# Low parts of the first-layer weights all on GpSimd, and the token-counting products behind the first-layer product

## The chip, the cores and the metric

The kernel runs on one core of a Trainium2 chip. A time is the device's microseconds (us) for one execution; the median of three runs of the kernel before is 858.86 us (857.1 to 858.91). The engines are TensorE (PE; PEld is its loading of weights), VectorE (DVE), ScalarE (ACT), GpSimd (POOL) and SyncE (SP). Each works through its own list of instructions in order; an instruction that waits holds up all that stand behind it on the same engine.

## The reference

Three stages follow each other. The third, to which the change belongs, is:

```python
def _moe2_ref(x, w_gate, w1, w2):          # x 3072x384, 8 experts, w1 384x1024, w2 1024x384
    cap = N // E                           # 384 tokens for each expert
    order = np.argsort(-(x @ w_gate).flatten())
    for idx in order:                      # greedy: best logit first, an expert closes at cap
        tok, e = idx // E, idx % E
        if assigned[tok] >= 0 or counts[e] >= cap: continue
        assigned[tok] = e; counts[e] += 1
    for e in range(E):
        mask = assigned == e
        out[mask] = np.maximum(x[mask] @ w1[e], 0.0) @ w2[e]
```

Ahead of it stand a gated linear attention over 32 heads and 768 positions, and a dense pair of layers (384 to 2048 to 384) with a squared relu.

## The kernel before

Attention and the dense layers fill the first 568 us or so. Then the expert stage begins. Experts are found one after the other: a search (function `search`, line 836) narrows a threshold in five rounds until some expert is full; which one closes next is known only then. The eight experts that are found are called k = 0 to 7, in that order. While expert e is computed, expert k = e + 1 is searched, loaded and prepared.

**Products.** All weights and activations are float32 split in two float32r parts, a high one (a rounded copy) and a low one (the rest); each product is high by high, high by low and low by high. Expert e takes eight steps s. A step is nine first-layer products (`layer1`, L993, 128x384 each, into `ph`), the relu on ACT (L1001) and the low part of its result on DVE (L1002), and nine second-layer products of the step two earlier (`layer2`, L1011, three for each third i of the tokens). The first-layer products take the low parts of the weights as they go: the sixth of the nine is the first to read the low part of the third piece.

**Weights.** For each expert POOL issues an indirect load of w1 (L742, into `w1s`) and w2 (L746, into `w2s`), as soon as the search has named it and the one buffer of each is free. `split_w` (L946) then makes the two parts of seven pieces: 0 to 2 of w1 (128x1024) and 3 to 6 of w2 (128x768). "h" is the high part, on ACT (L956); "p" the low part on POOL and "d" the low part on DVE (both L958).

**Tokens.** `slots` (L767) turns the mask of an expert's tokens into a list of rows, in ten steps: two products that count tokens (L771 and L772, into `pp`, which read the mask `mk` and its running sum `mi`), a chain of small DVE operations (L775 to L783), three DVE comparisons of 128x1024 (`spot`, L790, into `lh`) with small products (L799), 24 small products (L807, into `po`), the row numbers (L811 to L820), and last the gather of the tokens (L764, three indirect DMAs on POOL into `xg`). `expert_x` (L960) transposes the three gathered tiles on PE (L966, "x0" to "x2") and splits them on ACT and DVE (L967, L968).

**Order.** The order of the stage is written out by hand in tables. An entry (r, p, "...") puts operations at place p of step r; r counts steps from the start of the expert before k, so 0 to 7 lie in expert k-1 and 8 to 15 in expert k itself. Places 0 and 1 are around the first-layer products, 2 is behind relu, 3 to 5 follow the three thirds of the second layer. "s" is a step of the search, "t" of `slots`; "e", "w" are the copy and the indirect write of a third of an expert's output (L1016, L1019). `STEADY` orders search and slots of k = 2 to 7, `FIRST` those of k = 1; `EXTRA` the preparation of k = 1 to 5, `EXTRA6` and `EXTRA7` that of k = 6 and 7; `OUT` the output of every expert. The function `side` (L1048) looks them up:

```python
for k, r in ((e + 1, s), (e, s + FT2), (e - 1, s + 2 * FT2)):
    for a in PLAN[3 if k == 1 else min(max(0, k - E + 3), 2)].get((r, p), "").split():
        if a == "s":   next(rest, None)
        elif a == "t": next(SL[k], None)      # where slots of k has begun
        ...
        elif a[0] == "w": write(k, i)
        else: split_w(k, i, a[:-1])
```

Of the kernel before, what the change touches and what calls it, by code (L numbers as in the profile page):

```python
# [41 lines left out]
def table(entries):  # L42
    at = {}
    for r, p, what in entries:
        at[r, p] = at.get((r, p), "") + " " + what
    return at
# [1 line left out]

STEADY = ((0, 0, "s"), (0, 1, "s"), (0, 3, "s"), (0, 4, "s"), (0, 5, "s"), (1, 1, "s"), (1, 3, "s"), (1, 5, "t"),
# [3 lines left out]
OUT = (17, 3, "e0"), (17, 4, "e1"), (17, 5, "e2"), (18, 2, "w0"), (20, 0, "w1"), (20, 5, "w2")  # L55
EXTRA = ((4, 2, "h0"), (4, 4, "h1"), (5, 3, "d0 h2"), (6, 0, "h3"), (6, 3, "x0"), (6, 4, "p2 p1"), (7, 3, "x2 p3"),
         (7, 4, "x1"), (7, 5, "h6"), (8, 0, "h4 p4"), (8, 2, "h5"), (8, 5, "p6"), (9, 2, "p5"))
EXTRA6 = ((5, 2, "h0"), (5, 3, "d0 h1"), (5, 5, "h2 d1"), (6, 2, "d2"), (6, 3, "x0"), (6, 4, "x1"), (6, 5, "x2"),
          (7, 1, "h3"), (7, 2, "h4 d3"), (7, 3, "h5 d4"), (7, 5, "h6 d5"), (8, 0, "d6"))
# [19 lines left out]
         (7, 3, "s"), (7, 4, "s"))  # L79
PLAN = [table(STEADY + OUT + e) for e in (EXTRA, EXTRA6, EXTRA7)] + [table(FIRST + OUT + EXTRA)]  # L80
FL = (2, 2, 1, 2)
# [1214 lines left out]
```

## Time and profile before

| | |
|---|---|
| profiled execution | 860.5 us, of which the span from first to last instruction is 858.7 |
| median of three runs | 858.86 us |
| mean granted TensorE clock | 0.972 |
| PE busy | 799.7 us, 93% of the span |
| DVE, ACT, POOL busy | 499.2, 339.5, 368.1 us |

A share of busy time is a mean over stages. In the expert stage one expert follows the other every 32 to 33 us, and what a change is worth there is read from the places where PE stands still within such a period. Matmuls overlap, so that a group of nine is shown as 1.75 to 1.83 us where the next group begins 1.6 us later.

### The profile page before, as it was taken

The page shows a single profiled execution, that of the slowest core. Times are in us where ns is not written, and L with a number is a line of the kernel's source. Part 1 is how long each engine was busy: PE and PEld are TensorE (multiplying, and loading weights), DVE is VectorE, ACT ScalarE, POOL GpSimd, SP SyncE. Part 2 cuts the span into 40 slices and gives each one's busy share as a digit, 9 for nine tenths or more (in the row PEclk, how much of TensorE's full clock was granted, in tenths as well). Part 3 has the DMA queues.
Part 4 walks back from the last instruction along what each step waited for, and adds up shares of the span by engine and source line. Part 5 has one row for each costly group of instructions (what it writes and reads, how often), then busy time and mean ns, then how long its engine had stood idle before and what let it go on. Part 6 is the DMA issues. An engine that isn't in the chain of part 4 may idle for free.

```text
span 858.7 us, 14480 instructions
## 1 busy us (share of the span) xinstructions
PE 799.7 (93%) x5752; PEld 753.1 (88%) x5752; DVE 499.2 (58%) x1150; ACT 339.5 (40%) x615; POOL 368.1 (43%) x351
## 2 busy tenths in 40 slices
PE   7688899999999999999999999986999899999993
PEld 6588898999999999999999999876788888889993
DVE  8898995444444435435433223476877877877730
ACT  2256463333234333233233345223436536536620
POOL 2355662342343343243242344225467577573411
PEclk9699999999999999999999999996999999999997
DMA  8455423112112112112100000041432522523510
GB/s 262 148 170 169 147 60 96 43 49 70 42 50 70 42 49 70 42 50 80 62 20 28 1 31 5 15 150 44 175 121 83 204 95 108 193 92 121 193 37 31
DMA packets 21627, 75.55 MB, mean 88 GB/s; under 512 B 3137, under 2 KB 10178, under 8 KB 19634
## 3 DMA queue, kind: packets, MB, share of 16 engines
q0 software_dynamic: 5520, 34.61, 11.0%
q1 hardware_dynamic: 11682, 25.72, 9.4%
q10 hardware_dynamic: 4352, 14.24, 5.6%
q8 instruction: 46, 0.75, 0.4%
q14 instruction: 27, 0.22, 0.1%
HBM read 63.84 MB, written 9.54 MB: 85 GB/s over the span
## 4 chain that ended last, share of the span: by engine, by line
PE 76%; DVE 14%; DMA 3%; ACT 3%; issue 2%; POOL 0%; SPq 0%; POOLq 0%; DVEq 0%; ACTq 0%
PE ph L389 22%; PE p L417 20%; PE ph L993 10%; PE py L1011 8%; DVE wbuf L958 3%; PE py L274 3%; PE psc L253 2%; PE p L672 2%; PE py L271 2%; DMA w1s<-in_moe_w_dram,wi 2%; ACT wbuf L956 2%; DMA akq<-in_akq_dram 2%; PE pn L293 1%; DVE suf L226 1%; DVE hl L1002 1%
## 5 line engine op out<-in xcount | busy, mean ns | idle before, releaser
L389 PE MATMUL ph<-xT,wbuf 128*128 128x384 f32 x1152 | 227.2, 341 | 9.9 <-DVE wbuf L460 7.7
L389 PEld LDWEIGHTS ph<-xT,wbuf 128*128 128x128 f32 x1152 | 204.7, 189 | 14.2 <-DVE wbuf L460 10.0
L417 PE MATMUL p<-wbuf,hl 128*128 128x392 f32 (+1 forms) x1008 | 202.3, 344 | 0.0
L401 DVE SCALAR_TENSOR_TENSOR s<-ph,s 128x384 f32<-128x384 f32 x112 | 62.2, 556 | 221.7 <-ACT s L394 221.7
L417 PEld LDWEIGHTS p<-wbuf,hl 128*128 128x128 f32 x1008 | 176.4, 188 | 1.7 <-issue 0.4
L405 POOL TENSOR_TENSOR hl<-s,hl 128x384 fp32r<-128x384 f32 x96 | 97.8, 1019 | 173.8 <-ACT hl L402 148.2
L394 ACT ACTIVATE s<-ph 128x384 f32<-128x384 f32 x128 | 63.1, 493 | 174.5 <-PE ph L389 133.3
L1011 PE MATMUL py<-wbuf,hl 128*128 128x384 f32 x576 | 124.3, 347 | 0.0
L993 PE MATMUL ph<-xt,wbuf 128*128 128x384 f32 x576 | 119.7, 352 | 1.3 <-DVE xt L968 0.9
L993 PEld LDWEIGHTS ph<-xt,wbuf 128*128 128x128 f32 x576 | 101.8, 193 | 4.7 <-DVE xt L968 2.3
L1011 PEld LDWEIGHTS py<-wbuf,hl 128*128 128x128 f32 x576 | 99.5, 189 | 0.1
L1001 ACT ACTIVATE hl<-ph 128x384 fp32r<-128x384 f32 x64 | 31.5, 492 | 113.2 <-PE ph L993 102.7
L402 ACT ACTIVATE hl<-s 128x384 fp32r<-128x384 f32 x96 | 50.4, 525 | 55.9 <-DVE s L401 54.8
L1002 DVE SCALAR_TENSOR_TENSOR hl<-ph,hl 128x384 fp32r<-128x384 f32 x64 | 35.4, 554 | 34.2 <-ACT hl L1001 33.5
L956 ACT ACTIVATE wbuf<-w1s 128x1024 fp32r<-128x1024 f32 x24 | 52.2, 2219 | 3.0 <-DMA w1s<-in_moe_w_dram,wi 3.0
L1019 POOL DMA_INDIRECT out_dram<-o,idx x24 | 30.5, 1270 | 52.0 <-ACT o L1016 18.4
L246 POOL TENSOR_TENSOR sad<-state,ae 48x192 f32<-48x192 f32 x40 | 27.0, 675 | 47.6 <-DVE state L310 36.9
L958 POOL TENSOR_TENSOR wbuf<-w2s,wbuf 128x768 fp32r<-128x768 f32 x24 | 43.7, 1846 | 4.4 <-ACT wbuf L956 4.4
L764 POOL DMA_INDIRECT xg<-x2d,row x24 | 23.0, 957 | 39.1 <-DVE idx L820 14.9
L958 POOL TENSOR_TENSOR wbuf<-w1s,wbuf 128x1024 fp32r<-128x1024 f32 x11 | 33.0, 3032 | 3.1 <-ACT wbuf L956 3.0
L357 POOL TENSOR_TENSOR wbuf<-wf,wbuf 128x384 fp32r<-128x384 f32 x16 | 18.3, 1141 | 37.3 <-ACT wbuf L356 37.2
L226 DVE TENSOR_TENSOR_SCAN suf<-akq,fresh 112x516 f32<-112x516 f32 x24 | 31.8, 1327 | 3.5 <-DMA akq<-in_akq_dram 2.9
(213 smaller groups left out, 1096.0 us busy)
## 6 DMA issues: line engine op xcount, KB each, us to landing
akq<-in_akq_dram ACTq DMA_DIRECT2D x16, 677.2 KB, 4.6
rawi<-in_moe_w_in_dram SPq DMA_DIRECT2D x16, 384.0 KB, 3.1
rawo<-in_moe_w_out_dram SPq DMA_DIRECT2D x16, 384.0 KB, 3.8
akq<-in_akq_dram SPq DMA_DIRECT2D x7, 677.2 KB, 5.8
x2d<-xo SPq DMA_DIRECT2D x24, 192.0 KB, 2.2
v<-in_v_dram ACTq DMA_DIRECT2D x16, 192.0 KB, 2.7
v<-in_v_dram SPq DMA_DIRECT2D x8, 192.0 KB, 5.2
xf<-xf SPq DMA_DIRECT2D x16, 72.0 KB, 3.1
```

Source lines behind the costliest of these rows:

```text
L226: dve.tensor_tensor_scan(back(one(P)), back(one(al)), back(one(fresh)), 1.0, op0=OP.mult, op1=OP.add)
L389: pe.matmul(ph[:, :UT], win[:, wi, kt, fs], XT[u][:, xi, kt, :], start=n == 0, stop=n == 3 * KT - 1)
L394: act.activation(s, ph[:, :UT], AF.Relu)
L401: dve.scalar_tensor_tensor(s, ph[:, :UT], 0.0, s, op0=OP.max, op1=OP.mult)
L402: act.activation(hl[:, 0], s, AF.Copy)
L405: (dve if u == 0 or (u, f) == (NU - 1, FT - 1) else pool).tensor_tensor(hl[:, 1], s, hl[:, 0].bitcast(F32), op=OP.subtract)
L417: pe.matmul(PY[u][t][:, :w], hl[:, si, t * C:(t + 1) * C], wout[:, wi, f, :w], start=f == 0 and n == 0, stop=f == FT - 1 and n == 2)
L956: act.activation(dst[:, 0], src, AF.Copy)
L958: (dve if "d" in e else pool).tensor_tensor(dst[:, 1], src, dst[:, 0].bitcast(F32), op=OP.subtract)
L993: pe.matmul(ph[:, :CAP], wa[:, wi, kt, j, :], xt[:, xi, kt, :], start=n == 0, stop=n == 3 * KT - 1)
L1002: dve.scalar_tensor_tensor(hl[:, 1], ph[:, :CAP], 0.0, hl[:, 0].bitcast(F32), op0=OP.max, op1=OP.subtract)
L1011: pe.matmul(PX[k, i][:, :DM], hl[:, hi_, i * 128:(i + 1) * 128], wb[:, wi, j, :], start=j == 0 and n == 0, stop=j == FT2 - 1 and n == 2)
```

## The change

Only the tables change:

```diff
-STEADY = (... (1, 3, "s"), (1, 5, "t"), (2, 0, "s t"), (2, 1, "t t"), (2, 4, "t"), (3, 3, "s"), (3, 5, "t s"), (4, 0, "t t t t"), ...)
+STEADY = (... (1, 3, "s"), (2, 0, "s"), (2, 1, "t"), (2, 3, "t t"), (2, 4, "t"), (2, 5, "t"), (3, 3, "s"), (3, 5, "t s"), (4, 0, "t t t t"), ...)
-OUT = (17, 3, "e0"), (17, 4, "e1"), (17, 5, "e2"), (18, 2, "w0"), (20, 0, "w1"), (20, 5, "w2")
+OUT = (17, 3, "e0"), (17, 4, "e1"), (17, 5, "e2"), (18, 2, "w0"), (20, 0, "w1"), (22, 2, "w2")
-EXTRA = ((4, 2, "h0"), (4, 4, "h1"), (5, 3, "d0 h2"), (6, 0, "h3"), (6, 3, "x0"), (6, 4, "p2 p1"), (7, 3, "x2 p3"),
+EXTRA = ((4, 2, "h0"), (4, 4, "h1"), (4, 5, "p0"), (5, 2, "p1"), (5, 3, "h2"), (6, 0, "h3 p2"), (6, 3, "x0"), (7, 3, "x2 p3"),
```

The low part of piece 0 of k = 1 to 5 goes from DVE ("d0") to POOL ("p0"); p0, p1 and p2 stand earlier in POOL's list. The last third of an expert's output is written two steps later. For k = 2 to 7 the counting products stand behind the nine first-layer products of step 2 instead of ahead of them, and the DVE work that follows them stands behind L1002 of that step. `FIRST`, which orders k = 1, is not changed, and has its last step of `slots`, the gather, at (6, 1).

POOL's list where k = 1 is prepared (w1s and w2s are the loaded weights, wbuf_65 the split ones of k = 1, xg the gathered tokens):

```order
 L742 DMA w1s<-in_moe_w_dram,wi 128x3072
 L746 DMA w2s<-in_moe_w_dram,wi 128x3072
-L764 DMA xg<-x2d,row 128x384 x3
-L958 TENSOR_TENSOR wbuf_65<-w1s,wbuf_65 128x1024 x2
+L958 TENSOR_TENSOR wbuf_65<-w1s,wbuf_65 128x1024 x3
+L764 DMA xg<-x2d,row 128x384 x3
 L958 TENSOR_TENSOR wbuf_65<-w2s,wbuf_65 128x768 x4
```

Three low parts stand in front of the gather, where the gather stood in front of two. For k = 2 to 5 the gather stays in front:

```order
 L764 DMA xg<-x2d,row 128x384 x3
-L1019 DMA out_dram<-o,idx 3072x384 x2
-L958 TENSOR_TENSOR wbuf_64<-w1s,wbuf_64 128x1024 x2
-L958 TENSOR_TENSOR wbuf_64<-w2s,wbuf_64 128x768 x4
-L742 DMA w1s<-in_moe_w_dram,wi 128x3072
-L746 DMA w2s<-in_moe_w_dram,wi 128x3072
-L1019 DMA out_dram<-o,idx 3072x384
-L764 DMA xg<-x2d,row 128x384 x3
-L1019 DMA out_dram<-o,idx 3072x384 x2
-L958 TENSOR_TENSOR wbuf_65<-w1s,wbuf_65 128x1024 x2
+L1019 DMA out_dram<-o,idx 3072x384
+L958 TENSOR_TENSOR wbuf_64<-w1s,wbuf_64 128x1024 x3
```

There, one of the two output writes has moved from ahead of the low parts to a place behind the first three of them.

DVE's list at step 2 of an expert, where the chain of `slots` begins (x, r, b, lh and rh are its intermediate tiles; hl is the relu's low part):

```order
 L933 TENSOR_TENSOR um<-um,na 128x24
+L1002 SCALAR_TENSOR_TENSOR hl_6334<-ph_6321,hl_6334 128x384
 L775 SCALAR_TENSOR_TENSOR x<-mk,pp 128x24
 L778 TENSOR_SCALAR b<-x 128x24 x2
```

```order
 L799 TENSOR_TENSOR rh<-iopc,b 128x24x2 x3
-L790 TENSOR_TENSOR lh<-r_6329,ioslot 128x1024
-L1002 SCALAR_TENSOR_TENSOR hl_6352<-ph_6334,hl_6352 128x384
-L790 TENSOR_TENSOR lh<-r_6329,ioslot 128x1024
+L790 TENSOR_TENSOR lh<-r_6347,ioslot 128x1024 x2
 L1002 SCALAR_TENSOR_TENSOR hl_6380<-ph_6370,hl_6380 128x384
```

The relu's low part of step 2 stood between the second and third comparison and now stands ahead of the whole chain.

## Rows read from the trace of the kernel before

**Rows 1.** The page: busy time of TensorE, and its granted clock.

```profile
PE 799.7 (93%) x5752; PEld 753.1 (88%) x5752; DVE 499.2 (58%) x1150; ACT 339.5 (40%) x615; POOL 368.1 (43%) x351
...
PEclk9699999999999999999999999996999999999997
```

**Rows 2.** Waits of PE, 620 to 850 us: total, times, longest.

```profile
PE pc L874 <- DVE cm L866: 6.2, 5, 1.3
PE pp L771 <- DVE wi L740: 3.2, 5, 1.0
```

**Rows 3.** Timeline 674 to 692, k = 3: start, us, work, idle before.

```profile
681.01 1.00 POOL L1019 DMA_INDIRECT out_dram<-o,idx  x1 [0.43 <-issue]
...
682.48 2.24 DVE L958 TENSOR_TENSOR wbuf<-w1s,wbuf 128x1024 fp32r<-128x1024 f32 x1
...
684.29 0.69 PE L1011 MATMUL py<-wbuf,hl 128*128 128x384 f32 x3
...
685.19 0.95 DVE L866 TENSOR_TENSOR cm<-m,pc 128x768 bf16<-128x768 f32 x1
...
686.20 0.31 PE L874 MATMUL pc<-oh,cm 128*128 128x32 bf16 x6 [1.23 <-DVE cm L866]
```

**Rows 4.** Timeline 611 to 621.5, where k = 1 is prepared.

```profile
611.66 4.19 ACT L956 ACTIVATE wbuf<-w1s 128x1024 fp32r<-128x1024 f32 x2 [2.08 <-DMA w1s<-in_moe_w_dram,wi]
...
613.15 0.95 POOL L764 DMA_INDIRECT xg<-x2d,row  x1 [6.68 <-DVE steps L901]
...
615.67 0.95 POOL L764 DMA_INDIRECT xg<-x2d,row  x1 [0.30 <-issue]
...
618.47 3.29 POOL L958 TENSOR_TENSOR wbuf<-w1s,wbuf 128x1024 fp32r<-128x1024 f32 x1 [1.86 <-ACT wbuf L956]
618.48 0.69 PE L1011 MATMUL py<-wbuf,hl 128*128 128x384 f32 x3
...
620.66 0.53 PE L966 MATMUL px<-ident,xg 128*128 128x128 f32 x3
```

**Rows 5.** Groups by line, 620 to 850 us: busy us, mean ns, idle before.

```profile
L958 POOL TENSOR_TENSOR wbuf<-w1s,wbuf 128x1024 fp32r<-128x1024 f32 x10 | 30.2, 3050 | 2.0 <-ACT wbuf L956 1.9
```

**Rows 6.** DMA issues, 612.9 to 617 us: KB each, median us to landing.

```profile
xg<-x2d,row POOLq DMA_INDIRECT x3, 3.0
```

**Rows 7.** The tile xg, 600 to 660 us.

```profile
DMA to landing us min/median/max: 2.9/3.3/4.4
```

**Rows 8.** Stretches: us, busy of PE, PEld, DVE, ACT, POOL, clock, DMA, GB/s.

```profile
576.00:580.00 4.00, 1.40 (x10) 0.70 (x9) 2.55 (x5) 4.00 (x3) 3.09 (x4) 1.00 0.76 245
580.00:584.00 4.00, 0.51 (x8) 0.28 (x8) 3.51 (x7) 3.30 (x3) 2.84 (x2) 0.77 0.61 196
584.00:588.00 4.00, 3.38 (x24) 3.23 (x24) 2.22 (x7) 0.84 (x1) 4.00 (x3) 0.50 0.03 12
```

**Rows 9.** Timeline 692 to 708, steps 0 to 3 of the next expert.

```profile
694.12 5.44 POOL L958 TENSOR_TENSOR wbuf<-w2s,wbuf 128x768 fp32r<-128x768 f32 x3 [0.84 <-ACT wbuf L956]
...
700.49 0.17 PE L771 MATMUL pp<-mi,onesb 128*128 128x24 bf16 x1 [0.55 <-DVE wi L740]
...
701.26 0.17 DVE L775 SCALAR_TENSOR_TENSOR x<-mk,pp 128x24 f32<-128x24 bf16 x1
...
702.41 0.49 ACT L1001 ACTIVATE hl<-ph 128x384 fp32r<-128x384 f32 x1 [1.94 <-PE ph L993]
...
706.36 0.55 DVE L1002 SCALAR_TENSOR_TENSOR hl<-ph,hl 128x384 fp32r<-128x384 f32 x1
...
706.97 0.76 PE L807 MATMUL po<-rh,lh 128*128 128x6 bf16 x24
```

**Rows 10.** Line 919 on DVE, 570 to 860 us: ns min/median/max.

```profile
L919 DVE SCALAR_TENSOR_TENSOR ez<-cz,ioe x6: 166/168/557, 602.5 to 764.7; 128x8 f32<-128x8 f32 x6
```

**Rows 11.** DVE, 666 to 668 us.

```profile
666.54 0.56 DVE L919 SCALAR_TENSOR_TENSOR ez<-cz,ioe 128x8 f32<-128x8 f32 x1
```

**Rows 12.** POOL, 659 to 672 us.

```profile
659.83 7.25 POOL L958 TENSOR_TENSOR wbuf<-w2s,wbuf 128x768 fp32r<-128x768 f32 x4
```

More of the change, by code (lines that the diff above doesn't have):

```diff
@@ L46, in table @@
     return at
-STEADY = ((0, 0, "s"), (0, 1, "s"), (0, 3, "s"), (0, 4, "s"), (0, 5, "s"), (1, 1, "s"), (1, 3, "s"), (1, 5, "t"),
[1 row of a table removed]
+STEADY = ((0, 0, "s"), (0, 1, "s"), (0, 3, "s"), (0, 4, "s"), (0, 5, "s"), (1, 1, "s"), (1, 3, "s"), (2, 0, "s"),
[1 row of a table added]
           (4, 4, "s"), (4, 5, "s"), (5, 1, "s s"), (5, 3, "s"), (5, 5, "s"), (6, 0, "s"), (6, 3, "s"), (6, 4, "s"),
           (6, 5, "s"), (7, 1, "s"), (7, 3, "s"), (7, 4, "s"))
-OUT = (17, 3, "e0"), (17, 4, "e1"), (17, 5, "e2"), (18, 2, "w0"), (20, 0, "w1"), (20, 5, "w2")
-EXTRA = ((4, 2, "h0"), (4, 4, "h1"), (5, 3, "d0 h2"), (6, 0, "h3"), (6, 3, "x0"), (6, 4, "p2 p1"), (7, 3, "x2 p3"),
+OUT = (17, 3, "e0"), (17, 4, "e1"), (17, 5, "e2"), (18, 2, "w0"), (20, 0, "w1"), (22, 2, "w2")
+EXTRA = ((4, 2, "h0"), (4, 4, "h1"), (4, 5, "p0"), (5, 2, "p1"), (5, 3, "h2"), (6, 0, "h3 p2"), (6, 3, "x0"), (7, 3, "x2 p3"),
          (7, 4, "x1"), (7, 5, "h6"), (8, 0, "h4 p4"), (8, 2, "h5"), (8, 5, "p6"), (9, 2, "p5"))
```

2 rows, old and new, of the table STEADY are left out of this document.

## The prediction

> **What bounds the kernel now.** I read the page first: TensorE is busy 93% of the span, and its granted clock is full in all but a few slices [rows 1]. So time is gained where PE stands still and lost where it is made to. Next I read PE's waits in the expert stage: two kinds repeat once per expert, five times each. The search's products L874 wait for the DVE comparison L866 (6.2 us in all, 1.2 each), and the counting products wait for DVE (3.2 us in all) [rows 2]. The timeline of one period shows why the first is there: the low part d0 holds DVE for 2.24 us from 682.48, the comparison comes only at 685.19, and PE, done at 684.98, starts at 686.20 [rows 3]. In the second, PE waits 0.55 at 700.49 [rows 9]. Last I read the same places for k = 1, which has its own table, because there POOL's list changes order: gather at 613.15 to 615.67, low parts from 618.47, transposes of the gathered tokens at 620.66 [rows 4].
>
> **k = 1: the gather goes behind three low parts.** POOL can begin p0 when the first high part is done. ACT makes two in 4.19 us from 611.66, so the first is ready at 613.75 [rows 4]. A low part takes 3.05 us on POOL [rows 5], so p0 to p2 end at 613.75 + 9.15 = 622.9. Only then is the gather issued, though its row numbers are ready before 613.15. Its third DMA begins 2.52 after its first [rows 4], at 625.5, and lands 3.0 later here [rows 6], at 628.5. PE's list has the transposes in step 6, and each needs all three tiles' landing to go past. PE has d0's wait removed and is there at 618.48 + 0.69 = 619.2 [rows 4]. It stands until 628.5, and all products behind are held with it. Against 620.66 before, that is **+7.85 us**. From both sides: a landing of 2.9 gives 7.75, one of 4.4 gives 9.25 [rows 7]; a low part of 3.29, as the one at 618.47 [rows 4], gives 0.7 more. Nothing hides it: PE is the bound on both sides of the stall, and what it did not do in 9.3 us has to be done later.
>
> **The clock.** A stall of 9.3 us has one like it in the trace. From 576 to 584 PE was busy 1.91 of 8 us; within 580 to 584 the granted clock fell to half (mean 0.77), and from 584 to 588, with PE at work 3.38 of 4 us, it was still 0.50 [rows 8]. That is 1.2 in place of 2.4 GHz. So I expect about 4 us of PE's work after the stall at half speed, which costs half of it: **+2.0 us**. Bounds: 0, if the clock holds; 5, if it stays low for 10 us, since the slice from 580 to 601 has a mean of only 0.6 [rows 1].
>
> **k = 2 to 5: d0 leaves DVE.** Without the 2.24 us the comparison is done before PE needs it, and the wait of 1.23 goes: four of the five waits, -4.9 us in all [rows 2, 3]. What is late next is POOL, below.
>
> **k = 2 to 7: the counting products.** Removed: a wait of 0.55 per expert. But the relu's low part L1002 now stands ahead of the whole chain on DVE. In the times of rows 9: ph starts 0.55 sooner, ACT's relu is at 701.86 instead of 702.41 and ends at 702.35, L1002 holds DVE until 702.85, and x, which was at 701.26, starts then. From x to the L1002 of step 3 lay 706.36 - 701.26 = 5.10, of which 0.47 was the L1002 that has gone ahead; so the third comparison ends at about 702.85 + 4.63 + 0.08 = 707.55. PE would be at the 24 products at 706.97 - 0.55 = 706.42, can do 16 of them by 706.85, and waits 0.7 for the last comparison [rows 9]. The wait is not removed but moved: net +0.15 per expert, and the row numbers, with them the gather and p0 to p2, come some 0.8 to 1.2 later. Bounds: -0.55 per expert, if the comparisons are not waited for; +0.5, if the search's steps behind them are held up too. I take +0.2 for each of four.
>
> **k = 2 to 5: p0 on POOL.** It adds 3.05 us four times to an engine with free time, but shifts the end of its low parts. Before, the write at 681.01 ended at 682.01 and the last low part at 699.56 [rows 3, 9]. After: 682.0 + 0.8 (later row numbers) + 9.15 + 1.1 (the moved write) + 4 x 1.81 [rows 9] = 700.3. Two things hang on it. p2 ends at 682.8 + 9.15 = 691.95, and the sixth product of the next expert, now 1.0 sooner, wants it at about 692: no margin. And the end of the search, in which L919 and the running sum `mi` each read two tiles, runs at 698.4 to 699.5 instead of after POOL's end. L919 takes 0.168 us, but 0.557 in one case: that began at 666.54, while POOL's low parts ran until 667.08 [rows 10 to 12]. So a DVE operation of that kind waits for POOL's, and here `mi` would wait for the last low part until 700.3. Then the counting products wait again, by some 0.5, and the comparisons are 0.8 later.
>
> The Trainium skill says so too ("SBUF — State Buffer", Who interferes with whom): a VectorE instruction with two SBUF inputs contends with a GpSimd instruction that reads SBUF, and whichever starts first blocks the other; by that rule the four periods would gain nearly nothing, without it 4.0 us, and the 0.557 of rows 10 agrees with it. The Trainium skill's "GPSIMD Engine Reference" (Key points) has VectorE about twice as fast at elementwise work; by it p0 would take some 4.5 us, an estimate, and the stall of k = 1 would be 4 us longer, but the rows have 3.05 against 2.24, and they decide.
>
> So a period of k = 2 to 5 gains 1.2 - 0.2 = 1.0 if POOL disturbs nothing, and about 0.1 if each of these waits comes in full. I take 0.5, between the two: **-2.0 us** over four; bounds -4.9 and 0. The later write by itself delays nothing: its buffer is needed only an expert later.
>
> **The sum.** 7.85 + 2.0 - 2.0 = +7.85 us. The profiled execution takes 860.5 us (span 858.7 and 1.8 around it), so it would become 868.4. It lies 1.6 above the median of the runs, 858.86, from which I forecast 858.86 + 7.9 = **866.8 us**.
>
> **Rivals.**
> - *The clock holds and POOL disturbs nothing.* 7.75 - 4.9 + 0.8 = +3.7: 862.5 us. For it: PE's waits of 1.2 us per period leave the clock full in every slice of the expert periods [rows 1, 2]. Against: this stall is as long as the one of rows 8. Chance 0.12.
> - *POOL sets the pace.* p2 and `mi` are late in every period, d0's gain is lost, and k = 1 has the longer clock loss: 7.85 + 4 + 1 = +12.9: 871.7 us. For it: no margin for p2, and rows 10. Against: of six L919 only one is longer than the rest [rows 10], and p2's 0.05 us too little or too much is within what the working can tell. Chance 0.18.
> - *Faster: the gaps of the periods are worth more than the gather.* Both kinds of wait go in full, 4.9 + 3.2 = 8.1 [rows 2], and the stall of k = 1 is short. It decides from the point where the third gathered tile lands before 626.8, so that PE loses under 6.2 us: with POOL's low parts at 2.5 us each it would land at 626.8, and the time be 858.86 + 6.1 - 8.1 = 856.9. For it: the waits are there. Against: the mean of ten is 3.05 [rows 5]. Chance 0.05.
> - *The change does less than it says*, as POOL's gather could go past its low parts: then k = 1 loses nothing. Against: the list has it behind them, and an engine goes through its list in order. It would end at 855 to 859; its chance, 0.03, is split between faster and same.
>
> **How the numbers follow.** The forecast has 0.62, its own range 863 to 870. The range of 0.8 takes in the first rival's time and part of the second's: 862 to 872.5. A difference under 0.2% (1.7 us) can't be told from no change. Slower has the forecast, the first two rivals: 0.92. Same 0.03, faster 0.05.
>
> **What would show it.** In the trace of the changed kernel: for k = 1, three low parts on POOL from 613.8, the gather from about 622.9, and PE still until about 628.5 with a wait for `xg` at L966; a granted clock of 0.5 in some us around 626 to 633; for k = 2 to 5 no wait of L874 for L866; the wait of the counting products gone or smaller, and a new one of L807 for the comparisons of 0.5 to 0.8; L919 or L922 lengthened on DVE. The prediction is wrong if PE reaches the transposes of k = 1 before 626, or if the periods of k = 2 to 5 come under 31 us.

## The result, and the profile after

The changed kernel takes 870.84 us (median of four, 868.84 to 875.85) against 858.88 for the kernel before on the same chip; the ratio is 1.0145, with a 95% interval of 1.0113 to 1.0177. It is 12 us slower; 866.8 was forecast, with a range of 862 to 872.5. The profiled execution took 868.84 us, with a span of 867.0. It comes to the preparation of k = 1 2.4 us earlier than the profiled execution of before, by differences in a stretch that the change does not touch (the steps of expert 0 ahead of them), so places are compared by their distance from a common point.

POOL's timeline for k = 1 (start, us, work, idle before):

```profile
611.35 8.97 POOL L958 TENSOR_TENSOR wbuf<-w1s,wbuf 128x1024 fp32r<-128x1024 f32 x3 [7.27 <-ACT wbuf L956]
620.47 0.97 POOL L764 DMA_INDIRECT xg<-x2d,row  x1
621.74 0.95 POOL L764 DMA_INDIRECT xg<-x2d,row  x1 [0.30 <-issue]
623.00 0.95 POOL L764 DMA_INDIRECT xg<-x2d,row  x1 [0.31 <-issue]
```

PE's timeline from there on:

```profile
610.10 1.81 PE L993 MATMUL ph<-xt,wbuf 128*128 128x384 f32 x9
...
616.93 0.32 PE L874 MATMUL pc<-oh,cm 128*128 128x32 bf16 x6
623.61 0.48 PE L966 MATMUL px<-ident,xg 128*128 128x128 f32 x1 [6.37 <-DMA xg<-x2d,row]
624.81 0.48 PE L966 MATMUL px<-ident,xg 128*128 128x128 f32 x1 [0.72 <-DMA xg<-x2d,row]
625.93 0.47 PE L966 MATMUL px<-ident,xg 128*128 128x128 f32 x1 [0.65 <-DMA xg<-x2d,row]
...
628.54 3.20 PE L993 MATMUL ph<-xt,wbuf 128*128 128x384 f32 x9
...
638.08 1.81 PE L993 MATMUL ph<-xt,wbuf 128*128 128x384 f32 x9
```

The three low parts run without a pause, the gather follows them, and PE waits 7.7 us for its three tiles (6.37, 0.72 and 0.65) where it waited for none [rows 4]. The nine products at 628.54 take 3.20 us where the others take 1.81: the clock. Stretches of 4 us (busy us of PE, PEld, DVE, ACT, POOL, then granted clock, DMA share and GB/s):

```profile
616.00:620.00 4.00, 1.25 (x13) 0.99 (x11) 1.48 (x4) 1.07 (x2) 4.00 (x2) 1.00 0.00 0
620.00:624.00 4.00, 0.39 (x1) 0.18 (x1) 0.00 (x0) 0.00 (x0) 3.22 (x5) 0.67 0.29 80
624.00:628.00 4.00, 2.63 (x12) 1.94 (x12) 0.84 (x3) 0.49 (x1) 1.78 (x1) 0.50 0.21 67
628.00:632.00 4.00, 4.00 (x16) 3.64 (x14) 1.44 (x4) 0.22 (x1) 0.00 (x0) 0.55 0.00 0
632.00:636.00 4.00, 4.00 (x35) 3.58 (x34) 2.84 (x10) 2.72 (x5) 0.11 (x1) 1.00 0.00 0
```

The granted clock fell to half, 1.2 GHz, while PE stood still and came back only near 632, some 6 us after the last transpose began. Before, the nine products that stand at 610.10 here began at 612.49 and those of 638.08 at 630.60, as PE's timeline of before shows:

```profile
612.49 1.81 PE L993 MATMUL ph<-xt,wbuf 128*128 128x384 f32 x9
...
630.60 1.81 PE L993 MATMUL ph<-xt,wbuf 128*128 128x384 f32 x9
```

From the one to the other it was 630.60 - 612.49 = 18.11 us and is 638.08 - 610.10 = 27.98: **9.9 us lost**. The last transpose ends 625.93 + 0.47 - 610.10 = 16.30 us behind the first point; before, the three ended 620.66 + 0.53 - 612.49 = 8.70 behind it [rows 4]. So 7.6 us are lost by the transposes and 2.3 behind them. The 7.6 is the waits of 7.7 and what the transposes take more one by one (1.4 us against 0.5) and 0.3 us that PE loses ahead of them, less the wait of L874 (1.3 us before), which went.

In the periods of k = 2 to 5 the waits changed places. PE's waits from 620 to 850 us, to be set against [rows 2]:

```profile
PE px L966 <- DMA xg<-x2d,row: 7.7, 3, 6.4
PE po L807 <- DVE lh L790: 3.8, 6, 0.7
PE pp L771 <- DVE wi L740: 1.8, 3, 0.9
...
PE pc L874 <- DVE cm L866: 0.5, 1, 0.5
```

L874's 6.2 us have become 0.5, the counting products' 3.2 have become 1.8, and a new wait of 3.8 stands at the 24 products. Here it is, in two periods:

```profile
680.93 0.56 PE L807 MATMUL po<-rh,lh 128*128 128x6 bf16 x16
682.18 0.35 PE L807 MATMUL po<-rh,lh 128*128 128x6 bf16 x8 [0.69 <-DVE lh L790]
...
713.55 0.56 PE L807 MATMUL po<-rh,lh 128*128 128x6 bf16 x16
714.83 0.35 PE L807 MATMUL po<-rh,lh 128*128 128x6 bf16 x8 [0.72 <-DVE lh L790]
```

Sixteen are done and eight wait for the third comparison. The period is 713.55 - 680.93 = 32.62 us: from the same product at 674.33 to the one at 706.97 [rows 9] it was 32.64 before. And the search's end waits for POOL, as the timeline of all engines around 673 shows:

```profile
671.58 3.65 POOL L958 TENSOR_TENSOR wbuf<-w2s,wbuf 128x768 fp32r<-128x768 f32 x2
673.68 1.58 DVE L919 SCALAR_TENSOR_TENSOR ez<-cz,ioe 128x8 f32<-128x8 f32 x1
...
676.04 0.17 PE L771 MATMUL pp<-mi,onesb 128*128 128x24 bf16 x1 [0.38 <-DVE wi L740]
```

L919, an operation of 0.17 us [rows 10], ends when POOL's low parts end, at 675.2. In the four periods it takes 0.89 to 2.07 us. So they gain nothing: the first nine products behind the 24 of one expert and those of the expert four later lie 130.90 us apart before (641.86 to 772.76) and 130.98 here (649.49 to 780.47). The period behind these even grows, from 28.71 to 29.52 us. It makes the tokens of k = 7, whose counting products did not wait before; moved behind the nine products, they make the 24 products late (PE's timelines, the first row of before, the second of the changed kernel):

```profile
800.85 0.76 PE L807 MATMUL po<-rh,lh 128*128 128x6 bf16 x24
...
809.78 0.35 PE L807 MATMUL po<-rh,lh 128*128 128x6 bf16 x8 [0.49 <-DVE lh L790]
```

### The profile page after: what moved, and what is told of

Its sections match the earlier page's. It is cut to its first block, busy times and chain, and to the rows that moved or that the text cites. A ratio compares the mean times of both kernels' runs of the same rounds, so it can differ in the third digit from the quotient of the medians.

```text
span 867.0 us, 14496 instructions
## 1 busy us (share of the span) xinstructions
PE 800.8 (92%) x5752; PEld 752.2 (87%) x5752; DVE 496.3 (57%) x1145; ACT 340.0 (39%) x615; POOL 381.1 (44%) x356
## 4 chain that ended last, share of the span: by engine, by line
PE 72%; DVE 17%; DMA 4%; issue 3%; POOL 1%; ACT 1%; SPq 0%; POOLq 0%; DVEq 0%; ACTq 0%
PE ph L389 22%; PE p L417 20%; PE ph L993 7%; PE py L1011 7%; PE p L672 3%; PE psc L253 3%; PE py L274 2%; DVE lh L790 2%; PE py L271 2%; DMA akq<-in_akq_dram 2%; DVE hl L1002 1%; DVE wbuf L958 1%; PE pn L293 1%; DMA xg<-x2d,row 1%; DVE cm L866 1%
## 5 line engine op out<-in xcount | busy, mean ns | idle before, releaser
L993 PE MATMUL ph<-xt,wbuf 128*128 128x384 f32 x576 | 117.3, 347 | 1.0 <-DVE xt L968 0.9
L1002 DVE SCALAR_TENSOR_TENSOR hl<-ph,hl 128x384 fp32r<-128x384 f32 x64 | 35.4, 554 | 36.0 <-ACT hl L1001 34.9
L958 POOL TENSOR_TENSOR wbuf<-w1s,wbuf 128x1024 fp32r<-128x1024 f32 x16 | 47.8, 3013 | 8.6 <-ACT wbuf L956 8.4
L958 POOL TENSOR_TENSOR wbuf<-w2s,wbuf 128x768 fp32r<-128x768 f32 x24 | 43.5, 1844 | 10.7 <-ACT wbuf L956 10.6
L357 POOL TENSOR_TENSOR wbuf<-wf,wbuf 128x384 fp32r<-128x384 f32 x16 | 20.1, 1254 | 36.5 <-ACT wbuf L356 36.3
```

The costliest lines, as they stand in the source:

```text
L958: (dve if "d" in e else pool).tensor_tensor(dst[:, 1], src, dst[:, 0].bitcast(F32), op=OP.subtract)
L993: pe.matmul(ph[:, :CAP], wa[:, wi, kt, j, :], xt[:, xi, kt, :], start=n == 0, stop=n == 3 * KT - 1)
L1002: dve.scalar_tensor_tensor(hl[:, 1], ph[:, :CAP], 0.0, hl[:, 0].bitcast(F32), op0=OP.max, op1=OP.subtract)
```

## The experiments

**Which part costs.** The first run gives k = 1 its old table and keeps the rest of the change; the second does only what the first takes away.

```diff
 # first run: the changed kernel, and
+EXTRA1 = ((4, 2, "h0"), (4, 4, "h1"), (5, 3, "d0 h2"), (6, 0, "h3"), (6, 3, "x0"), (6, 4, "p2 p1"), ...   # as before
-... [table(FIRST + OUT + EXTRA)]
+... [table(FIRST + OUT + EXTRA1)]
 # second run: the kernel before, with EXTRA1 = the new EXTRA
```

> The changed kernel, but k = 1 has its old table (d0 on DVE, gather ahead of p2 and p1). Theory (the gather of k = 1 behind three low parts costs 9.9 us, 7.6 of stall and 2.3 of clock, and the periods of k = 2 to 5 gain 0.1 each): 858 to 860 us, no wait of L966 for xg, no fall of the clock after 600 us. Rival (the low parts on GpSimd in every period are what costs, and the stall of k = 1 is only where it shows): 865 us or more.

> The kernel before, but k = 1 alone has the new order of the low parts (p0, p1, p2 ahead of its gather). Theory: all of the loss is here, 868 to 870 us, PE without work for 9 us at the transposes of k = 1, clock at half for 7 to 10 us after. Rival (the periods cost): within 3 us of before, 859 to 862.

The first took 860.05 us, ratio to before 1.0017 (0.9990 to 1.0045); no wait of L966 is left among PE's waits, the granted clock is full from 600 us on, and the waits of L807 (4.0 us) and of the counting products (3.2) are there as in the changed kernel (3.8 and 2.1 from 600 us on). The second took 871.24 us, ratio 1.0121 (1.0068 to 1.0173), 1.2 us above the upper end expected, with this at the transposes:

```profile
628.05 0.47 PE L968 MATMUL px<-ident,xg 128*128 128x128 f32 x1 [6.25 <-DMA xg<-x2d,row]
```

So all of the loss that can be measured is k = 1's, and the periods of k = 2 to 5 gain nothing that can be measured. The rival's 865 us or more is out; a cost of the periods of some 0.4% is not.

**The two halves of the change for k = 2 to 5.** Both with k = 1 as before; the third run has the old `STEADY` under the new `EXTRA` and `OUT`, the fourth the new `STEADY` alone.

```diff
 # third run: the first run, and
-STEADY = (... (2, 0, "s"), (2, 1, "t"), (2, 3, "t t"), (2, 4, "t"), (2, 5, "t"), ...
+STEADY = (... (1, 5, "t"), (2, 0, "s t"), (2, 1, "t t"), (2, 4, "t"), ...
 # fourth run: the kernel before, with the new STEADY
```

> k = 1 as before, search and slots in the old order; only the low parts of k = 2 to 5 are all on GpSimd and the last output write is late. Theory (L919 waits for GpSimd's last low part, about 1.1 us, and the counting products wait for it): the wait of L874 is gone, that of the counting products 1.5 us or more instead of 0.55, 858 to 860 us. Rival (the later comparisons, behind L1002, take the gain of d0): here they stand as before, so four periods gain 1.2 each, 854 us.

> The kernel before with only the new order of slots for k = 2 to 7 (counting products behind the nine products of step 2). Theory (the wait is moved to the 24 products behind the third comparison): the wait of L771 gone, one of L807 of 0.5 to 0.7 per expert, 859 to 861 us. Rival (the 0.55 us per expert is gained): 856 us.

The third was a surprise: 876.92 us, ratio 1.0181 (1.0125 to 1.0238), slower by far than both expectations. The timeline of all engines shows why:

```profile
679.47 1.01 POOL L1021 DMA_INDIRECT out_dram<-o,idx  x1 [0.30 <-PE ph L995]
...
679.87 9.43 DVE L882 TENSOR_TENSOR ee<-oh,ioe 128x192 f32<-128x192 bf16 x1
...
680.50 8.57 POOL L960 TENSOR_TENSOR wbuf<-w1s,wbuf 128x1024 fp32r<-128x1024 f32 x3
...
689.21 0.55 DVE L1004 SCALAR_TENSOR_TENSOR hl<-ph,hl 128x384 fp32r<-128x384 f32 x1
...
689.88 0.17 PE L894 MATMUL pb<-full,later 128*128 128x8 bf16 x1 [8.28 <-DVE full L892]
```

(The line numbers are two higher than in the kernel before: L882 is its L880, the search's product of `oh` and `ioe`, which reads two SBUF tensors.) It takes 0.35 us where it meets no low part and 9.43 here: it ends with the third of POOL's low parts and not with the first, and PE stands 8.3 us. This happened in two of the four periods (679.87 and 755.36); in the others (645.52 and 720.90) it took 0.35. The granted clock fell to half behind both. In these two the product begins 0.40 us after POOL began to issue the output write that stands right ahead of p0, and 0.63 us ahead of p0; in the other two it begins ahead of that issue, 1.4 us ahead of p0. In the changed kernel the later row numbers keep p0 1.5 to 2.0 us behind it: for k = 2 to 5 the two halves of the change need each other. My theory for this run (only L919 waits) fell.

The fourth took 862.39 us, ratio 1.0025 (0.9995 to 1.0055), 1.4 above the theory's 859 to 861 and far from its rival's 856. The counting products' wait is down to 0.2 us, and L807's is 3.4:

```profile
PE pc L874 <- DVE cm L866: 4.5, 5, 1.3
PE po L807 <- DVE lh L790: 3.4, 6, 0.7
```

**Is it what the DVE operation reads?** The eighth run is the third with one operand moved: `ioe` is copied to PSUM first.

```diff
+ids = pc[:, G * E + T:G * E + T + E]
+dve.tensor_copy(ids, ioe)
-dve.tensor_tensor(ee, oh, ioe[:, None, :].to_broadcast(eb), op=OP.mult)
+dve.tensor_tensor(ee, oh, ids[:, None, :].to_broadcast(eb), op=OP.mult)
```

> The third experiment (only the low parts moved, 877 us) with L880 alone given an input in PSUM. Theory (L880 read two SBUF tensors and waited 9.4 us for the three low parts that GpSimd makes without a pause): L880 takes 0.3 to 0.4 us everywhere, the waits of L892 for L890 of up to 8 us go, 858 to 861 us. Rival (DVE is held up by GpSimd whatever it reads): L880 or its neighbours as long as in that run, 870 us or more.

It took 863.44 us, ratio 1.0032 (1.0010 to 1.0055): 13 us less than the third run, and all seven products take 0.35 us (ns min/median/max):

```profile
L884 DVE TENSOR_TENSOR ee<-oh,pc x7: 353/355/355, 554.2 to 744.7; 128x192 f32<-128x192 bf16 x7
```

POOL's work and its order are the same, and the product comes as close to p0 as in the third run (679.95, with p0 at 680.26). So it is the second SBUF input that makes a DVE operation wait for POOL's low parts; the seventh run, below, shows it within one low part. It is 2.4 us above the upper end expected; L919 and the counting products behind it still wait there, 8.3 us in all, as the theory for the third run had it.

**What the periods would gain without those waits.** The sixth run is the first with three operations on one SBUF input (L880 as in the eighth run, L919, L922); the seventh also puts the small chain of slots ahead of L1002 again; the ninth frees the rest of the search's end.

```diff
 # sixth
+nil = pz[:, 2 * E:2 * E + NCH]
+dve.memset(nil, 0.0)
-cz = sm.tile([128, E], F32, name="cz", bufs=2)
+cz = pz[:, E:2 * E]
-dve.tensor_tensor_scan(mi, mk, zero24, 0.0, ...)
+dve.tensor_tensor_scan(mi, mk, nil, 0.0, ...)
 # seventh, also
-(2, 1, "t"), (2, 3, "t t")
+(2, 1, "t t"), (2, 3, "t")
 # ninth, also
-dve.scalar_tensor_tensor(wi, ek, 128.0, iopw, op0=OP.mult, op1=OP.add)
+dve.tensor_scalar(wi, ek, 128.0, iopw, op0=OP.mult, op1=OP.add)
-dve.tensor_tensor(esum, esum, ek, op=OP.subtract)
+dve.tensor_scalar(esum, esum, ek, None, op0=OP.subtract)
-pen = sm.tile([128, E], F32, name="pen", bufs=2)
+pen = pz[:, 64:64 + E]
-na = sm.tile([128, NCH], F32, name="na", bufs=2)
+na = pz[:, 128:128 + NCH]
```

> The first experiment (k = 1 as before) with three DVE operations given one input in PSUM instead of two in SBUF: L880 (ioe copied to PSUM first), L919 (cz made in PSUM), L922 (zeros in PSUM). Theory (two SBUF inputs make them wait for GpSimd's low parts): L919 falls from 1.7 to about 0.2 us, the wait of the counting products goes, each of four periods gains up to 1.0: 856 to 858 us. Rival (GpSimd's own lateness holds the period, through its loads or p2): no change, 860 us.

> The run before with the small operations L775 to L783 again ahead of L1002 of step 2: entry (2, 1) has two steps of slots. Theory (the third comparison ends 0.7 us too late for the 24 products): the wait of L807 for L790 goes, 0.6 for each of five experts, 853 to 855 us. Rival (another of DVE's results is then late): as the run before.

The sixth took 857.76 us, ratio 0.9982 (0.9959 to 1.0004), the seventh 857.45, ratio 0.9972 (0.9946 to 0.9997). The counting products no longer wait in the sixth. But L740, the next operation with two SBUF inputs, has taken the wait over: 133/472/1105 ns in the sixth, and in the seventh

```profile
689.61 7.22 POOL L964 TENSOR_TENSOR wbuf<-w2s,wbuf 128x768 fp32r<-128x768 f32 x4
...
695.66 0.20 DVE L928 TENSOR_TENSOR_SCAN mi<-mk,pz 128x24 bf16<-128x24 bf16 x1
695.78 1.08 DVE L742 SCALAR_TENSOR_TENSOR wi<-ek,iopw 128x1 int32<-128x1 f32 x1
```

(L742 there is L740 of before, L928 is L922.) L928, with one of its two inputs in PSUM, takes its 0.20 us while the last low part runs; L742, with both in SBUF, ends with that low part. The chain behind it is late, and L807 still waits 3.4 us in all; so the seventh missed its expectation.

> The seventh experiment with the rest of the search's end freed too: L740 takes iopw as a scalar, pen and na lie in PSUM, esum is lowered by a scalar. In the two runs before, L740, which reads two SBUF tensors, took over the wait (up to 1.1 us). Theory (two SBUF inputs): L740 back to 0.13 us, the wait of the 24 products for the third comparison under 0.3, 853 to 855 us as a median. Rival (what is left is GpSimd's lateness by order): 857 us, as that run.

The ninth took 855.18 us, ratio 0.9940 (0.9919 to 0.9961), faster than both kernels and 0.2 above the upper end expected. L740 is at 0.19 us everywhere, four times of eight within a low part, and PE's waits from 600 us on are half of what they were (5.3 us in all, 11.2 before):

```profile
L742 DVE TENSOR_SCALAR wi<-ek,iopw x8: 186/188/193, 570.3 to 792.0; 128x1 int32<-128x1 f32 x8
```

```profile
PE pb L891 <- DVE rc L879: 1.4, 6, 0.3
PE pc L876 <- DVE cm L868: 1.0, 1, 1.0
PE ph L999 <- DVE xt L974: 0.9, 1, 0.9
PE po L809 <- DVE lh L792: 0.7, 3, 0.3
```

The four periods that take 130.90 us before take 124.88 here.

Do the operands alone bring this? The tenth run is the kernel before with the same edits to them.

> The kernel before, with the same DVE operations on one SBUF input and nothing else changed. Theory (before, only one L919 waited, 0.4 us, so the operands are worth little by themselves): within 1.5 us of before. Rival (the forms with an input in PSUM are faster or slower in themselves): 2 us or more either way.

It took 860.77 us, ratio 1.0016 (0.9987 to 1.0044): no gain.

**One low part ahead of the gather.** The fifth run is the changed kernel with the gather of k = 1 at (5, 0), behind p0 alone.

```diff
-(5, 0, "t s s"), ... (6, 0, "s"), (6, 1, "t"), ...
+(5, 0, "t s s t"), ... (6, 0, "s"), ...
```

> The changed kernel, but in the table of k = 1 the last step of slots stands at (5, 0): the gather is behind one low part, not three. Theory (the stall is as long as the low parts ahead of the gather make it): third tile lands 6 us sooner, PE waits some 3 us instead of 7.7, the clock does not fall, 862 to 864 us. Rival (any low part ahead of the gather brings the stall and the clock's fall): 867 us or more.

It took 866.35 us, ratio 1.0073 (1.0046 to 1.0099). PE waits 2.2 us for the gather instead of 7.7, so the stall goes with the low parts ahead of it. But the clock fell all the same, which I had excluded:

```profile
620.00:624.00 4.00, 1.81 (x15) 1.17 (x13) 1.22 (x4) 0.77 (x2) 3.67 (x3) 1.00 0.50 141
624.00:628.00 4.00, 4.00 (x19) 3.54 (x19) 2.19 (x7) 0.49 (x1) 4.00 (x3) 0.57 0.00 0
```

So the time is between what the theory and its rival gave. By the profile k = 1 costs 3.3 us here (from the first nine products behind its 24 to those of the next expert 32.70 us, before 29.37); of the 5.4 us that this profile loses from the first of these points to its end, the rest lies in the later periods. No run has all three low parts of k = 1 on POOL behind its gather.

## Why the prediction was right, and where a term was off

- **k = 1, the gather behind three low parts: right.** Predicted 7.85 us by the transposes, measured 7.6. PE did not stand for 9.3 us in one piece, as the text had it, but did each transpose when its tile had landed, with 7.7 us of waits between; the last tile decides all the same. The edit alone costs 1.2% (second run), and taking it away brings the time back to that of before (first run).
- **The clock after the stall: right in kind, and near in size.** 2.0 predicted; 9.9 - 7.6 = 2.3 from the profile. The slow stretch began before PE was back, and PE worked some 5.5 us of it (626.06 to about 631.6) instead of 4; half of that would be 2.7, an estimate. Why it cost 0.4 less was not looked into.
- **d0 leaves DVE: right.** L874's wait fell from 6.2 to 0.5 us.
- **The counting products: right.** The wait was moved to the 24 products, 0.69 and 0.72 us where 0.7 was worked out; the fourth run shows it alone.
- **p0 on POOL: the mechanism right, the size too small.** I took 0.5 us of gain per period, between 1.0 and 0.1. The waits came in full: L919 took 1.58, 1.77, 0.89 and 2.07 us, and the first run is at 1.0017 where -2.0 us would be 0.9977. The step that was mis-sized is "I take 0.5, between the two: -2.0 us over four": it measured about zero, the end that the text gave for the waits in full, and that is half of the 4 us between the forecast and the measured time. By the rule that the prediction cited from the Trainium skill ("SBUF — State Buffer", Who interferes with whom) the four periods would gain nearly nothing, and so it came. The eighth and ninth runs bear out its condition, two SBUF inputs. That whichever starts first blocks the other is not borne out by the recorded starts of the third run, where L880 starts 0.63 us ahead of p0 and is the one that waits.
- **Not in the sum: k = 6 and 7.** The counting products move for k = 2 to 7, and +0.2 was taken "for each of four". The period that makes the tokens of k = 7 takes 0.8 us longer. In the profiles of all runs with the counting products behind the nine products it takes 29.28 to 29.76 us, in the others 28.71 to 28.83.
- **Missed: L880.** I looked at the search's end for operations with two SBUF inputs, and not at L880, 0.35 us long and just ahead of p0. In the changed kernel it is done in time for k = 2 to 5; in the third run it was not, at 8 us each time. For k = 1 it met the first low part in the changed kernel too, and took 2.10 us:

```profile
612.49 2.10 DVE L880 TENSOR_TENSOR ee<-oh,ioe 128x192 f32<-128x192 bf16 x1
```

It ended 0.2 us behind that low part, though two more followed without a pause, and PE came to its next nine products 0.3 us later for it (614.75 - 610.10 = 4.65 us, before 616.83 - 612.49 = 4.34). So it can be let in between two low parts; why it was not in the third run stays open, and so does what holds it there from 679.87 until p0's recorded start at 680.50. POOL was issuing a DMA then, but an issue alone does not hold it (at 655.89 in the changed kernel it took 0.35 us within one), and recorded times on POOL are rough.

- **The rest.** By the two profiles the change costs 9.9 us to the products at 638.08 and 228.9 - 228.1 = 0.8 from there to the end of the span: 10.7 where 7.85 was forecast. On the median of before that is 869.6 us, an estimate; the 1.3 us to the measured median are not accounted for, but the runs of the changed kernel spread from 868.84 to 875.85, and only the first of these was profiled. That the profiled execution, 868.84, is near the 868.4 worked out for one is in part luck: it has 2.4 us gained by chance ahead of k = 1.

## What to carry to other kernels

Before work is moved up in an in-order list, look at what it is put in front of in every table that uses the entry: here four experts were safe and the fifth had a gather, whose data PE waits for, behind 9 us of arithmetic. Work moved from DVE to GpSimd is not free for DVE: each small DVE operation with two SBUF inputs that meets it waits for the GpSimd operation that it meets (2.10 us in the changed kernel), and sometimes until GpSimd's whole unbroken run is over (9.43 us in the third run), so list those operations and give them an operand in PSUM or as a scalar (the ninth run, 0.6% faster than before, is the change with that done, the small chain of slots ahead of the relu's low part, and k = 1 left alone). And a gain of a wait counts only when the next result that the same engine needs is also there in time.

## What the runs showed of the hardware that was not expected

- A DVE operation with two SBUF inputs can fail to get in between two of POOL's operations that follow each other without a pause: twice in the third run L880 took 9.43 us, through three low parts of 8.57 us together, and L919 took 2.07 us in the changed kernel where one low part of that size takes 1.81. In other places it got in behind the first: L880 took 2.10 us in the changed kernel, as said above. What decides is not shown.
- One input in PSUM is enough to avoid it (the running sum took 0.20 us within a low part in the seventh run, L880 0.355 us right ahead of p0 in the eighth), and so is a scalar operand in place of a tensor (L740, 0.188 us, in the ninth run).
- The clock fell to half also after a stretch in which PE's longest single wait was 0.95 us (fifth run, 2.2 us of waits in all, 0.57 in the stretch after), and not after the waits of 1.2 us of the kernel before.
